# A written engine order replaced as a whole, the first query weights loaded in two pieces, and the last output products split

## The chip, the cores and the metric

The kernel runs on one core of a Trainium2 chip. The core has TensorE (PE, matrix products), VectorE (DVE), ScalarE (ACT), GpSimd (POOL) and SyncE (SP, which here only issues DMAs). The metric is device time in microseconds (us) of one execution, taken as the median of several runs. Alongside, a hardware profiler records one execution: its span runs from the first to the last recorded instruction.

## The reference

Two branches are computed and laid side by side. Branch A is attention with a memory, over 16 heads of width 28 and four segments of 512 rows:

```python
for s in range(N):                       # N = 4 segments, L = 512 rows
    qs, ks, vs = q[:, :, s], k[:, :, s], v[:, :, s]
    logits = jnp.einsum("bhqd,bhkd->bhqk", qs, ks) * scale + mask
    a_dot = jnp.einsum("bhqk,bhkd->bhqd", _softmax(logits), vs)
    pq = phi(qs)                         # phi(t) = t + 1 for t > 0, else exp(t)
    a_mem = einsum(pq, M) / (einsum(pq, z)[..., None] + 1e-6)
    outs.append(g * a_mem + (1.0 - g) * a_dot)      # g = sigmoid(beta)
    pk = phi(ks)
    M = M + jnp.einsum("bhld,bhle->bhde", pk, vs)
    z = z + jnp.einsum("bhld->bhd", pk)
return o @ wo                            # q, k, v = x @ wq, x @ wk, x @ wv
```

Branch B is a state-space convolution of `u` (448 channels, 2048 steps) by FFT, plus `u * D_skip`. All is float32.

## The kernel before, in words

**Units.** Branch A is cut into 16 units: unit t is segment s = t // 4 with a group g = t % 4 of four heads. Every operand of a projection is split into a high and a low part (`wh`/`wl`, `xh`/`xl`), and three products replace one exact one. A projection takes 11 products of 512 columns for the queries and as many for the keys of groups 0 to 2 (`P_proj`, L510), in a part of 6 and a part of 5; a tile of values takes 11 products of 448 columns (`V_tile`, L494).

**A unit's stages.** Score products L584 fill four PSUM banks at a time, in the array's row layout: a fill has blocks of 128 and 256 columns, or 384, or 512. VectorE takes the row maxima from these banks (L592). The maxima are transposed (L599), copied (L600) and written back into the queries. Exponent fills L615, again four banks each, of width 512, 384, and 256 with 128, are read by ScalarE, which makes the exponents P (L619, four instructions per fill); GpSimd sets the part above the diagonal to zero (L622). The products with the values L635 run in the column layout, and ScalarE copies the result (L638). For the memory there are transpositions L551, products L559, the update of M on VectorE (L567, L569) and the product of the mapped queries with M (L537). For the combination, the sums go through DRAM and come back as factors R; multiplications (L713), an addition (L717), a cast to `oh` (L719) and the remainder `ol` (L720) follow, on VectorE for units 13 and 14, on GpSimd for the others. Unit 15 does not go through DRAM: TensorE gathers the sums (L669), VectorE inverts them and applies the gate (L673, L676), TensorE spreads them again (L683, into column layout), and VectorE and ScalarE work in halves (L695 to L702). It does so first for the memory part, then for the dot part.

**Output.** When the four units of a segment are done, each of its four row tiles takes 12 products (`W_tile`, L731): three for each group (`oh` with `wh`, `oh` with `wl`, `ol` with `wh`). ScalarE copies the tile (L737) and SP stores it (L739).

**Branch B.** It runs on the other engines between: 16 tiles, each with a scale on ScalarE (L792), a scan on VectorE (L794), the carried column and the final sum on GpSimd (L796, L799) and a second scale on ScalarE (L797). One buffer, `sc`, serves all the scans. The limits up to which the scan stands for the convolution are worked out on VectorE (L773 to L777), transposed by TensorE (L780) and made a flag; a general convolution behind that flag does not run here.

**What sets the order.** Each operation is recorded with its engine, its buffers and a cost (`Q.op`). The list `ORDER` numbers all of them, and the program is written in exactly that order for every engine and every DMA queue; each engine then takes its own instructions strictly in turn. The recorded costs have no influence on the written order. Buffers are handed out from small pools in the order of the list; the eight PSUM banks (tag `f`) serve everything that TensorE writes, so a fill waits until the engine that reads a bank's earlier contents is through.

**The beginning.** Four products of zeros warm TensorE up (L825). The first input chunks and the first key and query weights are loaded (L449 for weights, L464 for input), cast on ScalarE (L450, L466) and split on VectorE (L453 for weights, L469 and L472 for input). Six small instructions on VectorE (L407 to L412) work out the gates.

## Time and profile before

| | |
|---|---|
| median of 3 runs | 333.07 us (332.98 to 333.58) |
| profiled execution | 333.07 us, span 331.4 us, so 1.67 us lie outside the span |
| TensorE clock granted | 0.998 |
| busy: TensorE, weight loads | 319.6 us (96%), 205.5 us (62%) |
| busy: VectorE, ScalarE, GpSimd | 212.1 us (64%), 217.0 us (65%), 150.1 us (45%) |
| DMA | 36.69 MB, 111 GB/s in the mean |

A matrix product's start is recorded, its end is modelled; since products overlap, the busy time of TensorE is more than the sum of their pitches. In rows of the timeline the first number is the start in us from the span's start, the second the time from the first start to the last end, then engine, line, operation, tiles and count; an idle time before the group and what ended it stand in brackets. In the groups by line the numbers behind the bar are busy time in us, mean ns of one, and idle time before them with its releasers. "PEld" is the load of weights into the array, beside the products.

### The profile page before, as it was taken

The numbers are of one execution on the slowest core, as the hardware profiler recorded it, in microseconds if no ns is written. First come the engines' busy times: TensorE is split into PE (matmuls) and PEld (weight loads), VectorE is DVE, ScalarE is ACT, GpSimd is POOL, SyncE is SP. The second block draws the span as 40 slices with busy tenths as digits, with TensorE's granted clock in tenths as the row PEclk, the third lists the DMA queues.
The fourth block names the chain that finished last, engine by engine and source line by source line (L and its number), as shares of the span: only waits on it lengthen the run. The fifth ranks groups of instructions, "written<-read, shape, count | busy, mean of one in ns | idle before, by whom it ended". The sixth has DMA issues, their size and how long they took to land.

```text
span 331.4 us, 7629 instructions
## 1 busy us (share of the span) xinstructions
PE 319.6 (96%) x2773; PEld 205.5 (62%) x2773; DVE 212.1 (64%) x692; ACT 217.0 (65%) x440; POOL 150.1 (45%) x196
## 2 busy tenths in 40 slices
PE   8999998999899999999999999999999999999992
PEld 3666774756555467657866557566766655557681
DVE  3778778988986887681487567762058368644250
ACT  4555687577788887887747667588533657575531
POOL 4024226446485746745956263534763063270200
PEclk9999999999999999999999999999999999999999
DMA  6665535254452264435542312215350301321203
GB/s 215 238 204 146 168 103 156 81 164 116 131 155 65 85 169 132 143 109 146 152 137 63 94 33 70 88 34 160 89 150 20 108 3 55 106 68 60 93 5 115
DMA packets 25144, 36.69 MB, mean 111 GB/s; under 512 B 7613, under 2 KB 12733, under 8 KB 25101
## 3 DMA queue, kind: packets, MB, share of 16 engines
q1 hardware_dynamic: 24492, 35.48, 36.1%
q10 hardware_dynamic: 608, 0.66, 0.6%
q8 instruction: 24, 0.39, 0.5%
q14 instruction: 20, 0.16, 0.2%
HBM read 21.35 MB, written 14.43 MB: 108 GB/s over the span
## 4 chain that ended last, share of the span: by engine, by line
PE 77%; DMA 5%; issue 4%; ACT 4%; DVE 4%; POOL 4%; ACTq 0%; SPq 0%; POOLq 0%; DVEq 0%
PE f L510 20%; PE f L584 12%; PE f L731 11%; PE f L615 10%; PE f L494 10%; PE f L635 9%; PE f L537 3%; DMA P<-in_wq 2%; POOL P L622 2%; ACT P L619 1%; DMA xin<-in_xT 1%; POOL u L799 1%; PE f L551 1%; DVE sc L794 1%; DVE f L592 1%
## 5 line engine op out<-in xcount | busy, mean ns | idle before, releaser
L592 DVE CUSTOM_DVE_ANT_0 f<-f,mask 128x128 f32<-128x128 f32 (+3 forms) x256 | 119.8, 517 | 57.7 <-PE f L584 56.0
L619 ACT ACTIVATE P<-f 128x384 f32<-128x384 f32 (+1 forms) x192 | 87.0, 534 | 19.3 <-PE f L615 18.3
L622 POOL TENSOR_SCALAR_AFFINE_SELECT P<-P 128x512 f32<-128x512 f32 x64 | 42.1, 671 | 76.6 <-ACT P L619 69.6
L615 PE MATMUL f<-q,k 29*128 29x256 f32 (+3 forms) x512 | 52.1, 460 | 0.6 <-ACT pvn L638 0.4
L584 PE MATMUL f<-k,q 28*128 28x384 f32 (+3 forms) x512 | 49.3, 461 | 0.1
L635 PE MATMUL f<-P,vb 128*32 128x128 f32 (+3 forms) x512 | 37.8, 435 | 1.4 <-POOL xl L469 0.8
L615 PEld LDWEIGHTS f<-q,k 29*128 29x128 f32 x512 | 27.3, 183 | 18.0 <-ACT P L619 6.1
L592 DVE DVE_READ_ACCUMULATOR2_ANT mx<- 128x1 f32 x256 | 36.0, 141 | 0.1
L713 POOL TENSOR_TENSOR pvn<-pvn,R 128x512 f32<-128x512 f32 x22 | 29.7, 1365 | 13.6 <-DMA R<-d 13.6
L635 PEld LDWEIGHTS f<-P,vb 128*32 128x32 f32 x512 | 15.8, 109 | 26.1 <-issue 17.4
L584 PEld LDWEIGHTS f<-k,q 28*128 28x128 f32 x512 | 21.7, 184 | 13.2 <-issue 5.8
L510 PE MATMUL f<-xh,wh_q 128*128 128x512 f32 x64 | 26.9, 420 | 1.1 <-DVE mx L592 0.9
L731 PE MATMUL f<-wh_o,oh 128*128 128x448 f32 x64 | 26.8, 418 | 0.0
L794 DVE TENSOR_TENSOR_SCAN sc<-ones,carry,sc 112x512 f32<-112x512 f32 x16 | 22.8, 1423 | 4.8 <-ACT sc L792 4.6
L494 PE MATMUL f<-wh_v,xh 128*128 128x448 f32 x64 | 25.8, 403 | 0.1
L510 PE MATMUL f<-xh,wl_q 128*128 128x512 f32 x64 | 25.4, 397 | 0.0
L799 POOL TENSOR_TENSOR u<-u,sc 112x512 f32<-112x512 f32 x16 | 20.6, 1285 | 9.5 <-DVE sc L794 4.2
L731 PE MATMUL f<-wh_o,ol 128*128 128x448 f32 x64 | 23.4, 366 | 0.0
L731 PE MATMUL f<-wl_o,oh 128*128 128x448 f32 x64 | 23.4, 366 | 0.0
L494 PE MATMUL f<-wl_v,xh 128*128 128x448 f32 x64 | 23.4, 365 | 0.0
L720 POOL TENSOR_TENSOR ol<-pvn,oh 128x512 fp32r<-128x512 f32 x13 | 16.7, 1281 | 13.7 <-ACT oh L719 13.7
L510 PE MATMUL f<-xh,wh_k 128*128 128x512 f32 x48 | 20.4, 424 | 0.2 <-DVE xh L472 0.2
(134 smaller groups left out, 521.0 us busy)
## 6 DMA issues: line engine op xcount, KB each, us to landing
R<-d SPq DMA_DIRECT2D x44, 128.0 KB
k<-q SPq DMA_DIRECT2D x16, 224.0 KB
u<-in_uT SPq DMA_DIRECT2D x16, 224.0 KB
out_y<-u SPq DMA_DIRECT2D x16, 224.0 KB
out_a<-os SPq DMA_DIRECT2D x16, 224.0 KB
xin<-in_xT SPq DMA_DIRECT2D x12, 256.0 KB
k<-k SPq DMA_DIRECT2D x12, 224.0 KB
P<-in_xT SPq DMA_DIRECT2D x4, 256.0 KB
```

Source lines behind the costliest of these rows:

```text
L494: nc.tensor.matmul(pv.ap, X(s, x, c).ap[:, cs], (wl if w else wh).ap[:, c], start=a, stop=b)
L510: nc.tensor.matmul(pp.ap, (wl if w else wh).ap[:, g, c], X(s, x, c).ap, start=a, stop=b)
L584: nc.tensor.matmul(bank[h].ap[:, c0:c0 + n], q.ap[rows(h), qb * P:(qb + 1) * P], k.ap[rows(h), 0:n], start=True, stop=True)
L592: nc.vector.tensor_tensor_reduce(sc, sc, mask[:, 512 - n:512], 1.0, -3.0e38, ALU.add, ALU.max, mx.ap[:, 4 * h + qb:4 * h + qb + 1])
L615: nc.tensor.matmul(bank[h].ap[:, c0:c0 + w], k.ap[rows(h, 29), kb * P:(kb + 1) * P], q.ap[rows(h, 29), P * kb:512], start=True, stop=True)
L619: Q.op("ACT", act(n), pri + 0.01 * h, lambda h=h: nc.scalar.activation(pb.ap[:, h, 0:n], bank[h].ap[:, 0:n], AF.Exp, scale=SCALE), r=[bank ...
L622: Q.op("POOL", 700, pri + 0.1, lambda c0=c0: nc.gpsimd.affine_select(pb.ap[:, :, c0:c0 + P], pb.ap[:, :, c0:c0 + P], [[0, 4], [1, P]], ALU ...
L635: nc.tensor.matmul(pvp.ap[32 * h:32 * h + 32, kb * P:512], VB(s, kb).ap[:, 4 * g + h, :], pb.ap[:, h, c0:c0 + 512 - P * kb], start=(kb == ...
L713: e.tensor_tensor(pvn.ap[:, i, :], pvn.ap[:, i, :], R.ap[:, 512 * i:512 * i + 512], ALU.mult)
L731: nc.tensor.matmul(po.ap, o.ap[:, cs], w.ap[:, g], start=(g == 0 and i == 0), stop=(g == 3 and i == 2))
L794: Q.op("DVE", 1354, pri, lambda: nc.vector.tensor_tensor_scan(sc.ap, ones.to_broadcast([112, 512]), sc.ap, cj, ALU.mult, ALU.add), r=[sc, ...
L799: Q.op("POOL", 1344, pri, lambda: nc.gpsimd.tensor_tensor(ut.ap, ut.ap, sc.ap, ALU.add), r=[ut, sc], w=[ut])
```

## The change

Three things change in what is recorded. The first query weights come in two loads on ACT's queue, 128 columns and then 384, each with its own cast and subtraction. The two query and key projections of unit 0 are recorded in four parts (3, 3, 3 and 2 products), so that they can alternate. In the last segment's output tiles the three products of unit 15's group become two operations: the two with `oh`, then the one with `ol`. Three recorded costs differ (800 to 700, 870 to 740, 1354 to 1560). The number of recorded operations goes from 1493 to 1504; TensorE's products are the same in number and shape. And the list `ORDER` is replaced from the first number to the last.

```diff
 ORDER = """
-73 0 11 1 2 8 23 5 14 20 21 54 17 22 27 42 12 24 74 13 30 3 45 4 48 9 10 6 102 7 55 56 15 98 16 18 19 28 103 29 99
+26 57 0 14 2 73 5 1 11 72 75 8 17 23 74 20 24 30 25 27 58 59 15 45 16 3 48 6 4 51 12 7 107 13 9 54 101 10 55 108 18
...
-        def load_w(nm, i, pri, eng="DVE", at=None, by="SP"):
+        def load_w(nm, i, pri, eng="DVE", at=None, by="SP", cs=range(4)):
             hi, lo = W[nm]
-            n = 512 if nm in "qk" else D
+            c0, n = P * cs[0], P * len(cs) if nm in "qk" else D
...
+            part = lambda z: flat(z.ap[:, i])[:, c0:c0 + n]
+            b, key = t if isinstance(t, tuple) else (t, 0)
+            t = (b, (key, c0)) if len(cs) < 4 else t
+            raw = lambda: b.ap[:, 512 * key + c0:512 * key + c0 + n]
+            at = [(i, c) for c in cs] if nm in "qk" else [i]
+            Q.op(by, 430, pri, lambda: (nc.sync if by == "SP" else nc.scalar).dma_start(raw(), src()[:, c0:c0 + n]), w=[t], land=-4 * P * n)
+            Q.op("ACT", act(n), pri, lambda: nc.scalar.copy(part(hi), raw()), r=[t], w=[(hi, a) for a in at])
...
-        def product(s, cost, pri, one, reads, out, hold):
-            for ii in (PASSES[0:6], PASSES[6:11]):
+        def product(s, cost, pri, one, reads, out, hold, cuts=(0, 6, 11)):
+            for ii in (PASSES[x:y] for x, y in zip(cuts, cuts[1:])):
...
-            product(s, r32(512), pri, one, [(wh, g), (wl, g)], pp, [d])
+            product(s, r32(512), pri, one, lambda cs: [(w, (g, c)) for w in (wh, wl) for c in cs], pp, [d],
+                    (0, 3, 6, 9, 11) if t == 0 else (0, 6, 11))
...
             for g in range(NG):
                 r = [] if s == 3 else [*st[4 * s + 3]["o"]]
-                r += [(o, lt // 2) for o in st[4 * s + g]["o"]]
-                Q.op("PE", 3 * r32(448), pri, lambda g=g: part(g), r=[(wh, g), (wl, g), *r], w=[po],
-                     hold=[os], mode="full")
+                oh, ol = ((o, lt // 2) for o in st[4 * s + g]["o"])
+                for ii, o in (((0, 1), [oh]), ((2,), [ol])) if 4 * s + g == 15 else (((0, 1, 2), [oh, ol]),):
+                    Q.op("PE", len(ii) * r32(448), pri, lambda g=g, ii=ii: part(g, ii), r=[(wh, g), (wl, g), *r, *o], w=[po],
+                         hold=[os], mode="full")
...
-            Q.op("DVE", 1354, pri, lambda: nc.vector.tensor_tensor_scan(
+            Q.op("DVE", 1560, pri, lambda: nc.vector.tensor_tensor_scan(
...
-        load_w("q", 0, -8.95, at=(z1, 0), by="ACT")
+        load_w("q", 0, -8.97, at=(z1, 0), by="ACT", cs=range(1))
+        load_w("q", 0, -8.95, at=(z1, 0), by="ACT", cs=range(1, 4))
```

Below, the places of the new list that matter here. A row gives its number on the engine, the line (those of the changed kernel lie 3 to 8 further on), the operation, what is written and what is read, with buffer numbers, and the size of what is written; `f_67` to `f_74` are the eight banks.

**The beginning, on VectorE.** `xh`/`xl` 78 to 81 and 86 to 88 are the four input chunks, `gt`, `ga`, `omg` and `mix` the gates. Before:

```order
3 L453 TENSOR_TENSOR wl_k<-P_102,wh_k 128x512
4 L375 TENSOR_REDUCE sel_155<-sel 128x1
5 L469 TENSOR_TENSOR xl_86<-P_101,xh_78 128x512
6 L469 TENSOR_TENSOR xl_87<-P_101,xh_79 128x512
7 L453 TENSOR_TENSOR wl_q<-P_102,wh_q 128x512
8 L407 TENSOR_SCALAR gt<-gt 128x20
9 L408 RECIPROCAL gt<-gt 128x20
10 L409 TENSOR_SCALAR ga<-gt 128x20
11 L410 COPY omg<-ga 128x4
13 L412 SCALAR_TENSOR_TENSOR mix<-mix,sel_155,omg 128x4
14 L469 TENSOR_TENSOR xl_88<-P_101,xh_80 128x512
15 L472 TENSOR_TENSOR xh_81<-P_101,xh_81 64x512
```

Now:

```order
3 L407 TENSOR_SCALAR gt<-gt 128x20
5 L408 RECIPROCAL gt<-gt 128x20
8 L411 TENSOR_TENSOR mix<-gt,omg 128x4
9 L412 SCALAR_TENSOR_TENSOR mix<-mix,sel_155,omg 128x4
10 L456 TENSOR_TENSOR wl_k<-P_102,wh_k 128x512
11 L472 TENSOR_TENSOR xl_86<-P_101,xh_78 128x512
12 L456 TENSOR_TENSOR wl_q<-P_102,wh_q 128x128
13 L472 TENSOR_TENSOR xl_87<-P_101,xh_79 128x512
14 L456 TENSOR_TENSOR wl_q<-P_102,wh_q 128x384
15 L472 TENSOR_TENSOR xl_88<-P_101,xh_80 128x512
16 L475 TENSOR_TENSOR xh_81<-P_101,xh_81 64x512
```

The gate instructions moved ahead of all splits, and the split of the first query weights is in two. On SP's queue, the gates' input moved to the head from behind the first three input chunks, the two loads of `ld` and `ds` that stood at the head moved behind the weights, and the four input chunks follow one another. TensorE takes key and query products of the same chunk alternately.

**Exponent fills, on TensorE.** L615 (now L620) are exponent fills, L584 (L589) score fills, L731 (L737) output products, L559 (L564) memory products. Unit 13 before:

```order
1162 L615 MATMUL f_67<-q_91,k_95 128x128
1163 L615 MATMUL f_71<-q_91,k_95 128x128
1164 L615 MATMUL f_74<-q_91,k_95 128x128
1165 L615 MATMUL f_70<-q_91,k_95 128x128
1166 L615 MATMUL f_68<-q_91,k_95 128x384
1167 L615 MATMUL f_72<-q_91,k_95 128x384
1168 L615 MATMUL f_71<-q_91,k_95 128x384
1169 L615 MATMUL f_74<-q_91,k_95 128x384
1170 L584 MATMUL f_69<-k_96,q_92 128x512
1171 L584 MATMUL f_70<-k_96,q_92 128x512
1172 L584 MATMUL f_73<-k_96,q_92 128x512
1173 L584 MATMUL f_67<-k_96,q_92 128x512
```

Unit 13 now, from behind the memory products that follow its 128 and 256 wide fill:

```order
1170 L737 MATMUL f_68<-wh_o,oh_111 128x448
1171 L737 MATMUL f_68<-wl_o,oh_111 128x448
1172 L737 MATMUL f_68<-wh_o,ol_116 128x448
1173 L620 MATMUL f_74<-q_91,k_95 128x512
1174 L620 MATMUL f_73<-q_91,k_95 128x512
1175 L620 MATMUL f_72<-q_91,k_95 128x512
1176 L620 MATMUL f_70<-q_91,k_95 128x512
1177 L737 MATMUL f_68<-wh_o,oh_112 128x448
1178 L737 MATMUL f_68<-wl_o,oh_112 128x448
1179 L737 MATMUL f_68<-wh_o,ol_117 128x448
1180 L589 MATMUL f_71<-k_96,q_92 128x384
1181 L589 MATMUL f_67<-k_96,q_92 128x384
```

Between the fills now stand output products, and the 384 wide one has moved behind the score fill. Unit 5 now, from the middle of its 128 and 256 wide fill on:

```order
491 L620 MATMUL f_68<-q_91,k_95 128x128
492 L620 MATMUL f_70<-q_91,k_95 128x128
493 L620 MATMUL f_72<-q_91,k_95 128x384
494 L620 MATMUL f_69<-q_91,k_95 128x384
495 L620 MATMUL f_73<-q_91,k_95 128x384
496 L620 MATMUL f_67<-q_91,k_95 128x384
497 L589 MATMUL f_70<-k_96,q_92 128x512
498 L589 MATMUL f_68<-k_96,q_92 128x512
499 L589 MATMUL f_71<-k_96,q_92 128x512
500 L589 MATMUL f_67<-k_96,q_92 128x512
501 L556 MATMUL f_72<-ident,phk_99 128x128 x4
502 L620 MATMUL f_69<-q_91,k_95 128x512
```

Here two exponent fills, a score fill and a transposition stand together; before, unit 5 had a 384 and a 512 wide exponent fill and a 128 and 256 wide score fill in a row.

**The end, on TensorE.** `oh`/`ol` 108 and 113 belong to unit 15; L669 (L674) gathers, L683 (L688) spreads. Before, for the dot part:

```order
1306 L731 MATMUL f_71<-wh_o,oh_111 128x448
1307 L731 MATMUL f_71<-wl_o,oh_111 128x448
1308 L731 MATMUL f_71<-wh_o,ol_116 128x448
1309 L669 MATMUL f_72<-pick,pvn_105 128x4 x4
1310 L731 MATMUL f_67<-wh_o,oh_111 128x448
1311 L731 MATMUL f_67<-wl_o,oh_111 128x448
1312 L731 MATMUL f_67<-wh_o,ol_116 128x448
1313 L683 MATMUL f_69<-ident,rr_133 32x128 x16
1314 L731 MATMUL f_68<-wh_o,oh_111 128x448
```

Now:

```order
1318 L737 MATMUL f_68<-wh_o,oh_111 128x448
1319 L737 MATMUL f_68<-wl_o,oh_111 128x448
1320 L737 MATMUL f_68<-wh_o,ol_116 128x448
1321 L674 MATMUL f_69<-pick,pvn_105 128x4 x4
1322 L688 MATMUL f_67<-ident,rr_133 32x128 x16
1323 L737 MATMUL f_74<-wh_o,oh_112 128x448
1324 L737 MATMUL f_74<-wl_o,oh_112 128x448
```

The three output products between gather and spread are gone from there. Behind the spread stand 24 output products instead of 33; twelve of the last 15 belong to unit 15, each two with `oh_108` followed by the one with `ol_113`.

**The limits, on VectorE.** The five instructions L773 to L777 (L780 to L784) stood between the maxima of unit 4's 384 wide and 512 wide score fills; now they stand among the four maxima of unit 5's 512 wide score fill. On TensorE the transposition of their result (L780, now L787) follows the second exponent fill of unit 3 behind that.

20 lines of the change are left out of this document (9 added, 11 removed), and 110 rows, old and new, of the table ORDER.

## The prediction

> **What bounds the kernel now.** I read the page first (busy shares, clock, chain), then TensorE's waits, then its timeline beside that of the engine it waits for.
>
> ```profile
> PE 319.6 (96%) x2773; PEld 205.5 (62%) x2773; DVE 212.1 (64%) x692; ACT 217.0 (65%) x440; POOL 150.1 (45%) x196
> ...
> PEclk9999999999999999999999999999999999999999
> ...
> PE 77%; DMA 5%; issue 4%; ACT 4%; DVE 4%; POOL 4%; ACTq 0%; SPq 0%; POOLq 0%; DVEq 0%
> ```
>
> TensorE is busy 96% at full clock and carries the chain; the others reach 65%. So the time is TensorE's own stream plus the holes in it. The 319.6 us overstate the stream: a product's modelled end lies after the start of the next, so part of a hole counts as busy. I therefore measure starts, not ends. The timeline of TensorE at one such hole (start, duration, engine, line, operation, tiles, count):
>
> ```profile
> 83.61 0.40 PE L510 MATMUL f<-xh,wl_k 128*128 128x512 f32 x1
> 83.94 1.14 PE L584 MATMUL f<-k,q 28*128 28x512 f32 x8
> 84.90 1.40 PE L615 MATMUL f<-q,k 29*128 29x512 f32 x8
> 87.20 0.50 PE L510 MATMUL f<-xh,wh_q 128*128 128x512 f32 x1 [0.90 <-DVE mx L592]
> 87.54 0.40 PE L510 MATMUL f<-xh,wl_q 128*128 128x512 f32 x1
> 87.77 0.40 PE L510 MATMUL f<-xl,wh_q 128*128 128x512 f32 x1
> ```
>
> and of VectorE there:
>
> ```profile
> 84.20 1.11 DVE L773 TENSOR_TENSOR mxa<-mxa,mxb 112x4 f32<-112x4 f32 x1
> ...
> 86.40 0.69 DVE L592 CUSTOM_DVE_ANT_0 f<-f,mask 128x512 f32<-128x512 f32 x1
> ```
>
> Eight score products of 512 columns fill four banks in 0.96 (83.94 to 84.90). The next eight, alike, are followed only after 2.30 (84.90 to 87.20), so 1.34 is lost, though only 0.90 is shown as idle. VectorE had 2.20 of scan-limit arithmetic (84.20 to 86.40) in front of a row maximum that empties a bank. The rows also price a change of array layout: within projections the pitch is 0.23 (87.54 to 87.77), but 0.33 into a score fill (83.61 to 83.94) and 0.34 after the return (87.20 to 87.54): 0.10 + 0.11 = 0.21 for each.
>
> Such holes, read the same way, are what an order can win: I find about 13.9 us, of which the parts below name the larger. The stream without them, which the change does not shorten except by layout changes, stays.
>
> **The start.** TensorE's first products and, below them, VectorE in the same stretch:
>
> ```profile
> 7.01 0.60 PE L510 MATMUL f<-xh,wh_k 128*128 128x512 f32 x1
> ...
> 11.59 0.50 PE L510 MATMUL f<-xh,wh_k 128*128 128x512 f32 x1 [0.22 <-DVE xh L472]
> ...
> 13.33 0.40 PE L510 MATMUL f<-xh,wh_k 128*128 128x512 f32 x1
> ```
>
> ```profile
> 8.86 0.17 DVE L407 TENSOR_SCALAR gt<-gt 128x20 f32<-128x20 f32 x1
> ...
> 10.13 0.68 DVE L469 TENSOR_TENSOR xl<-P,xh 128x512 fp32r<-128x512 f32 x1
> 10.84 0.69 DVE L472 TENSOR_TENSOR xh<-P,xh 64x512 fp32r<-64x512 f32 x1
> ```
>
> The first 22 products take 6.32 (7.01 to 13.33); at 0.233 each they need 5.13. The 1.19 lost lie just before the row at 11.59, where VectorE is still at the splits of the third and fourth input chunk because six gate instructions ran from 8.86 to 10.13 ahead of them. These six now come first, before any data has landed; their input, formerly fifth on SP's queue, heads it, and the two tiny scan loads no longer stand before the input chunks. The 128-column load costs one more DMA issue on ACT's queue, one short cast and one short subtraction, a few tenths in time those engines have spare; its earlier landing buys nothing by itself, since the warm-up products hold TensorE to about 7. I take the full -1.2; bounds 0 (a chunk lands late) and -1.5.
>
> By the page "TensorE: Matmul & The Clock Gate", section Back-to-back issue gap, 512 columns need about 216 ns in isolation. With it the 22 products would take 4.75 and this term would be -1.57. The row says 233 ns, and the row decides.
>
> **Layout changes.** Counted in both orders, 155 become 153: -0.4 at 0.21 each; bounds -0.6 and 0. The page "TensorEngine Tiling (Array Packing)", section Key Properties, says that changing tiling mode drains TensorE, and "TensorE: Matmul & The Clock Gate", Single matmul latency, gives a constant of about 0.17 us; two would then be worth 0.34. The trace agrees that a change costs something.
>
> **The limits.** They move off the place above, which frees 1.34. But now they stand between the first two and the last two maxima of a later 512-wide fill, and the short transposition of their result follows on TensorE, ahead of projections for the values. From that fill's start VectorE needs two maxima (0.69 at most), 2.20 of limits and another maximum, some 4.6 with the start-up; TensorE has 4.64 of work until there (0.96 fill, two-part projection 2.78, 0.03, 0.87 score fill), but the scan before the fill starts VectorE late by nearly a microsecond. New hole 0.9 (bounds 0, 1.8): net -0.45.
>
> **Fills drawn apart.** Three stretches of before (197 to 203, 275 to 278, 288 to 291) have two or three exponent fills with little between. The last of them on TensorE, and ScalarE in the middle one:
>
> ```profile
> 288.31 2.46 PE L615 MATMUL f<-q,k 29*128 29x384 f32 x22
> 290.93 0.47 PE L731 MATMUL f<-wh_o,oh 128*128 128x448 f32 x1
> ```
>
> ```profile
> 276.09 3.17 ACT L619 ACTIVATE P<-f 128x384 f32<-128x384 f32 x8 [0.92 <-PE f L615]
> ```
>
> ScalarE needs 0.38 for each 384-wide exponent (seven steps of 0.38 and a last 0.50 make the 3.17), TensorE about 0.7 for a fill that feeds four of them. Two fills in a row put 3 us on ScalarE behind 1.4 us of TensorE; the next fill finds its banks full. At 288.31 two fills worth 1.40 take 2.62: 1.22 lost. Summed the same way, the other two lose 1.4 and 1.5. In the new order, output products of 0.6 to 0.8 stand between these fills (the order's excerpt on unit 13); the same count leaves 0.5, 0.35 and 0.1. Gain 4.1 - 0.95, taken as -3.2; bounds -4.1 and -1.5.
>
> **Unit 5.** Here the new order does what it avoids elsewhere: 128/256 and 384 exponent fills, then a 512 score fill.
>
> ```profile
> 120.55 2.26 PE L615 MATMUL f<-q,k 29*128 29x384 f32 x15
> ...
> 124.12 0.47 PE L731 MATMUL f<-wh_o,oh 128*128 128x448 f32 x1
> ```
>
> From the groups by line and shape (count, busy total, mean ns, idle before and its releasers):
>
> ```profile
> L713 POOL TENSOR_TENSOR pvn<-pvn,R 128x512 f32<-128x512 f32 x22 | 29.7, 1365 | 13.6 <-DMA R<-d 13.6
> ...
> L792 ACT ACTIVATE sc<-u,c0t 112x512 f32<-112x512 f32 x16 | 11.6, 728 | 4.2 <-POOL carry L796 2.4 <-POOL u L799 1.1 <-DMA u<-in_uT 0.6
> ...
> L638 ACT COPY pvn<-f 128x512 f32<-128x512 f32 x16 | 9.3, 584 | 13.5 <-PE f L635 13.1 <-issue 0.5
> ```
>
> Before: 3.57 (120.55 to 124.12) for fills worth 2.36, so 1.2 lost. After: from the end of the value products ScalarE has a copy (0.58), a scale (0.73) and a relu, priced like the copy (0.3 less for all three, since one starts before the other's modelled end), then five exponents of 0.38 before the score fill has its first bank: 3.5, with start-ups 3.85. TensorE brings three fills of about 0.7. Lost 1.8, and 0.3 in the output products behind: +0.9; bounds 0 and +2.
>
> **Small rest.** The same count finds two shortfalls, 0.34 and 0.2, where before has none: +0.5; bounds 0 and +1.5. Gaps of before that no single queue explains are not credited.
>
> **The tail.**
>
> ```profile
> 315.55 1.05 PE L669 MATMUL f<-pick,pvn 128*128 128x4 f32 x8
> 316.46 0.45 PE L731 MATMUL f<-wh_o,oh 128*128 128x448 f32 x1
> ...
> 317.25 1.08 PE L683 MATMUL f<-ident,rr 128*32 128x128 f32 x32
> ...
> 324.77 0.37 PE L731 MATMUL f<-wh_o,ol 128*128 128x448 f32 x1
> ```
>
> Gather to spread takes 1.70 (315.55 to 317.25): gather products, reciprocal and gate factor on VectorE, then the spread. In it stands one output tile's 0.79 (316.46 to 317.25). The new order has the spread directly after the gather, so about 0.8 becomes a hole; the tile is done elsewhere. What follows shrinks from 33 output products to 24, and the chain from the spread to the last unit's first half must still fit: spread 1.08 and nine products of 0.2 cover 2.9; two multiplications and a sum of half width on VectorE and a cast on ScalarE need about as much. The split lets the first two products of a tile go before the low part is there; price without that cover 0.4. +0.8; bounds +0.3 and +1.3. Last copy and store stay as they are.
>
> **Sum.** -1.2 - 0.4 - 0.45 - 3.2 + 0.9 + 0.5 + 0.8 = -3.05. The profiled execution is 333.07, the median of the runs 333.07 as well: 330.0, span 328.3.
>
> **Rivals.** (1) *Given back* (0.15): the holes move rather than close. For it: before, 3.1 of 13.9 us of holes were of a kind that no single queue explains; against it, the start's 1.2 is plain. With the limits at 1.8, half the fill gain and unit 5 at +2: -1.2 - 0.4 + 0.45 - 1.6 + 2 + 0.5 + 0.8 = +0.55; taken 333.1 to 333.6, no change. (2) *Slower* (0.14): the scale instruction L792 waits for the one scan buffer, which GpSimd frees after a sum of its own, itself queued behind 1.37 products (L713, 22 of them); ScalarE then stands with exponents behind it and TensorE without banks. Before, its six such waits (2.4 + 1.1) hit little. In unit 5 it stands directly before eight exponents with about 0.5 to spare. One delay of a GpSimd product costs 1.37; from three of the 16 tiles on (4.1) it decides: 334.1. (3) *Order better than I count* (0.15): unit 5 and the tail take no more than before and the limits hide: -1.2 - 0.4 - 1.34 - 3.2 = -6.1, with the small rest 327.5. (4) *The split does nothing*: true already in my sum for the load; if input chunks land late too, the start gives 0 and the time is 331.2, inside the forecast's range.
>
> **Numbers.** Forecast 0.56 (own range 328.3 to 331.9). Likeliest 330.0; 8 in 10 from 327.4 to 333.8. 0.2%, or 0.67 us, is about what a measurement here tells from no change: faster 0.73 (forecast, better, and the edge of given back), same 0.12, slower 0.15.
>
> **What will show it.** Start: the 23rd product at 12.1 rather than 13.33. Limits: no hole near 85, one of about 0.9 at the flag's transposition. Units 9, 13, 14: exponents in fours of 1.64 with output products between. Unit 5: a hole of 1.8. Tail: spread 1.7 after gather with nothing between, last product 6.0 after that spread. Wrong if holes in the middle sum to more than 9 us, above all behind L792.

## The result

Over 20 runs each on one chip the kernel before takes 333.4 us (median) and the changed kernel 331.48 (330.58 to 334.74); the ratio is 0.9949, with a 95% interval of 0.9926 to 0.9971. So it is faster by about 1.7 us, with 1.0 to 2.5 as the interval (the medians lie 1.9 apart). On another chip, beside the last experiments, the unaltered changed kernel gave 331.97 and 0.9938 [0.9917, 0.9959]. Three of the 20 runs had a granted clock of 0.984 or 0.985 where the others had 0.994 to 0.998, and took 334.2 to 334.7.

The profiled execution took 331.92, span 330.2. Its page answers to the one of before as follows (busy time by engine, TensorE's granted clock over 40 slices, shares of the chain that ended last):

```profile
PE 316.8 (96%) x2773; PEld 205.4 (62%) x2773; DVE 216.6 (66%) x693; ACT 216.5 (66%) x441; POOL 151.8 (46%) x196
...
PE 82%; DVE 7%; ACT 4%; DMA 3%; issue 1%; POOL 0%; ACTq 0%; SPq 0%; POOLq 0%
```

TensorE carries more of the chain (82% for 77%), VectorE is busy 4.5 us longer although it got one small instruction more. The places where TensorE waits, from the view of waits of the changed kernel (engine, line, awaited engine, tile and line: total, times, longest):

```profile
PE f L514 <- POOL xh L475: 1.7, 1, 1.7
...
PE f L787 <- DVE mx L597: 1.3, 1, 1.3
PE f L620 <- DVE mx L597: 0.6, 1, 0.6
PE f L688 <- DVE rr L681: 0.6, 1, 0.6
```

These show the projections waiting for an input chunk, the flag's transposition, unit 5's exponent fills and the last spread. (Line numbers are now 3 to 7 higher: the maxima L592 are L597, the exponents L619 are L624, the products L713 and L720 are L718 and L725, the scale L792 is L799, the scan L794 is L801, the tiles' sum L799 is L806, the limits L773 to L777 are L780 to L784.)

Holes measured as in the prediction, start to start less the stream's own pitch, give this balance of the two profiled executions, one of each kernel:

| place | forecast | holes before | holes after | measured |
|---|---|---|---|---|
| start | -1.2 | 1.2 | 0.4, and the first product 0.2 later | -0.6 |
| layout changes (content of the stream) | -0.4 | | | -0.5 |
| limits | -0.45 | 1.34 | 1.35 | 0.0 |
| fills of units 9, 13, 14 | -3.2 | 4.1 | 0.9 | -3.2 |
| unit 5 | +0.9 | 1.2 | 2.6 | +1.4 |
| tail | +0.8 | 0.35 | 0.85 | +0.5, and 0.1 less behind the last product |
| all the rest | +0.5 | | | +1.3 |
| span | -3.05 | 331.4 | 330.2 | -1.2 |

The rest holds two numbers of opposite sign: 1.9 us at a place that has no hole before (the input chunk), and 0.6 us by which the other gaps shrank on balance. So the fills gain 3.2 and everything else together gives 2.0 of it back. That the two fewer layout changes are worth 0.5 is counted from the pitches; no run tries it by itself.

The largest forecast term came as worked out. Unit 14's last fills, TensorE and below it ScalarE:

```profile
287.07 0.82 PE L620 MATMUL f<-q,k 29*128 29x384 f32 x8
288.17 0.47 PE L737 MATMUL f<-wh_o,oh 128*128 128x448 f32 x1 [0.27 <-DVE mx L597]
```

```profile
287.96 1.64 ACT L624 ACTIVATE P<-f 128x384 f32<-128x384 f32 x4 [1.07 <-PE f L620]
```

A fill of eight stands alone now, exponents come in fours of 1.64, output products follow, and 0.35 is left of a hole of 1.22. No run moves these fills alone, but the reading repeats: the three stretches last 6.02, 3.60 and 2.61 us in both traces of the old order there (the kernel before and its variant with a new start, below), and where they stand in the new order, with the products between, 5.24, 4.36 and 4.33, the same to 0.02 us in all twelve traces of it.

### The profile page after: what moved, and what is told of

Same layout as the page of the kernel before. It is cut to its first block, busy times and chain, and to the rows that moved or that the text cites. A ratio compares the mean times of both kernels' runs of the same rounds, so it can differ in the third digit from the quotient of the medians.

```text
span 330.2 us, 7639 instructions
## 1 busy us (share of the span) xinstructions
PE 316.8 (96%) x2773; PEld 205.4 (62%) x2773; DVE 216.6 (66%) x693; ACT 216.5 (66%) x441; POOL 151.8 (46%) x196
## 4 chain that ended last, share of the span: by engine, by line
PE 82%; DVE 7%; ACT 4%; DMA 3%; issue 1%; POOL 0%; ACTq 0%; SPq 0%; POOLq 0%
PE f L514 20%; PE f L737 13%; PE f L589 11%; PE f L498 11%; PE f L620 10%; PE f L640 9%; DMA xin<-in_xT 3%; PE f L542 3%; DVE f L597 3%; ACT P L624 2%; PE f L832 2%; DVE sc L801 2%; PE f L556 2%; PE f L564 1%; PE f L688 1%
## 5 line engine op out<-in xcount | busy, mean ns | idle before, releaser
L597 DVE CUSTOM_DVE_ANT_0 f<-f,mask 128x256 f32<-128x256 f32 (+3 forms) x256 | 120.2, 514 | 58.4 <-PE f L589 56.6
L624 ACT ACTIVATE P<-f 128x384 f32<-128x384 f32 (+1 forms) x192 | 87.0, 532 | 18.3 <-PE f L620 16.9
L627 POOL TENSOR_SCALAR_AFFINE_SELECT P<-P 128x512 f32<-128x512 f32 x64 | 43.9, 699 | 85.4 <-ACT P L624 85.0
L620 PE MATMUL f<-q,k 29*128 29x256 f32 (+3 forms) x512 | 49.6, 459 | 0.6 <-DVE mx L597 0.6
L589 PE MATMUL f<-k,q 28*128 28x512 f32 (+3 forms) x512 | 48.7, 458 | 0.0
L620 PEld LDWEIGHTS f<-q,k 29*128 29x128 f32 x512 | 26.2, 183 | 16.5 <-issue 8.0
L597 DVE DVE_READ_ACCUMULATOR2_ANT mx<- 128x1 f32 x256 | 35.7, 140 | 0.1
L801 DVE TENSOR_TENSOR_SCAN sc<-ones,carry,sc 112x512 f32<-112x512 f32 x16 | 24.7, 1546 | 9.8 <-ACT sc L799 9.5
L718 POOL TENSOR_TENSOR pvn<-pvn,R 128x512 f32<-128x512 f32 x22 | 28.9, 1330 | 4.3 <-DMA R<-d 4.3
L589 PEld LDWEIGHTS f<-k,q 28*128 28x128 f32 x512 | 21.9, 184 | 13.0 <-issue 7.1
L806 POOL TENSOR_TENSOR u<-u,sc 112x512 f32<-112x512 f32 x16 | 21.0, 1310 | 14.5 <-DVE sc L801 7.3
L737 PE MATMUL f<-wh_o,oh 128*128 128x448 f32 x64 | 26.8, 419 | 0.3 <-DVE mx L597 0.3
L725 POOL TENSOR_TENSOR ol<-pvn,oh 128x512 fp32r<-128x512 f32 x13 | 16.7, 1287 | 14.9 <-ACT oh L724 13.2
L737 PE MATMUL f<-wh_o,ol 128*128 128x448 f32 x64 | 23.4, 366 | 0.0
L737 PE MATMUL f<-wl_o,oh 128*128 128x448 f32 x64 | 23.3, 365 | 0.0
```

Source lines behind the costliest of these rows:

```text
L589: nc.tensor.matmul(bank[h].ap[:, c0:c0 + n], q.ap[rows(h), qb * P:(qb + 1) * P], k.ap[rows(h), 0:n], start=True, stop=True)
L597: nc.vector.tensor_tensor_reduce(sc, sc, mask[:, 512 - n:512], 1.0, -3.0e38, ALU.add, ALU.max, mx.ap[:, 4 * h + qb:4 * h + qb + 1])
L620: nc.tensor.matmul(bank[h].ap[:, c0:c0 + w], k.ap[rows(h, 29), kb * P:(kb + 1) * P], q.ap[rows(h, 29), P * kb:512], start=True, stop=True)
L624: Q.op("ACT", act(n), pri + 0.01 * h, lambda h=h: nc.scalar.activation(pb.ap[:, h, 0:n], bank[h].ap[:, 0:n], AF.Exp, scale=SCALE), r=[bank ...
L627: Q.op("POOL", 700, pri + 0.1, lambda c0=c0: nc.gpsimd.affine_select(pb.ap[:, :, c0:c0 + P], pb.ap[:, :, c0:c0 + P], [[0, 4], [1, P]], ALU ...
L718: e.tensor_tensor(pvn.ap[:, i, :], pvn.ap[:, i, :], R.ap[:, 512 * i:512 * i + 512], ALU.mult)
```

## What held VectorE: the limits once more

In the changed kernel the limits stand at 95.77, and the flag's transposition waits for the maxima behind them. VectorE and GpSimd there:

```profile
95.77 1.60 DVE L780 TENSOR_TENSOR mxa<-mxa,mxb 112x4 f32<-112x4 f32 x1
97.29 0.15 DVE L781 TENSOR_TENSOR sai<-sai,sar 112x4 f32<-112x4 f32 x1
97.48 0.48 DVE L782 SCALAR_TENSOR_TENSOR lim<-mxa,sai 112x4 f32<-112x4 f32 x1
```

```profile
96.05 1.30 POOL L725 TENSOR_TENSOR ol<-pvn,oh 128x512 fp32r<-128x512 f32 x1
97.29 0.66 POOL L627 TENSOR_SCALAR_AFFINE_SELECT P<-P 128x512 f32<-128x512 f32 x1
```

An addition over 112 x 4 numbers takes 1.60, the next one of the same size 0.15. The long one ends at 97.37 where GpSimd's L725 ends (97.35), the third ends at 97.96 with GpSimd's L627 (97.95). In the kernel before it was the same, which the prediction did not look at. VectorE's second row there, and GpSimd:

```profile
85.24 0.66 DVE L774 TENSOR_TENSOR sai<-sai,sar 112x4 f32<-112x4 f32 x1
```

```profile
84.03 1.27 POOL L799 TENSOR_TENSOR u<-u,sc 112x512 f32<-112x512 f32 x1
85.25 0.63 POOL L622 TENSOR_SCALAR_AFFINE_SELECT P<-P 128x512 f32<-128x512 f32 x1
```

L773 (84.20 + 1.11) ends with L799 (84.03 + 1.27), L774 with L622. So the 2.20 of the prediction's "scan-limit arithmetic" was mostly waiting. The longest case in the changed kernel is a scan that takes 1.28 elsewhere:

```profile
109.50 3.54 DVE L801 TENSOR_TENSOR_SCAN sc<-ones,carry,sc 112x512 f32<-112x512 f32 x1
```

```profile
108.23 1.30 POOL L718 TENSOR_TENSOR pvn<-pvn,R 128x512 f32<-128x512 f32 x1
109.47 1.22 POOL L627 TENSOR_SCALAR_AFFINE_SELECT P<-P 128x512 f32<-128x512 f32 x2
110.66 1.29 POOL L725 TENSOR_TENSOR ol<-pvn,oh 128x512 fp32r<-128x512 f32 x1
```

GpSimd works without a gap until 111.95; the scan ends 1.09 later, about its own length. It began beside one GpSimd instruction, and three more were served before it. The instructions concerned (scans, limits, the factors rc, the mapped queries and keys) read two operands from SBUF; the maxima L597, which read a PSUM bank and a mask, are not lengthened beside GpSimd (the 64 of 128x512 take 0.67 to 0.73). Summed over all VectorE instructions that are more than 0.2 us above the usual length of their line and shape, the loss is 10.3 us before (17 instructions) and 14.2 after (20); the difference is most of VectorE's extra 4.5. In all 37 cases a GpSimd instruction was running when the long one began.

The Trainium skill, page "SBUF — State Buffer", section Who interferes with whom, says that a VectorE instruction with two SBUF inputs contends with a GpSimd instruction that reads SBUF, that contention for the shared ports is an exclusive lock, and (of VectorE's two-port modes) that whoever issues first has the ports for its whole instruction while the other is blocked fully. The trace agrees on the lock, with 1.60 for 0.15 and 3.54 for 1.28. It goes beyond the page in that one instruction lost to four in a row.

## Experiments

All are measured against the kernel before on the same chip. The edits of the order are shown as the numbers of the list, with the operation in brackets. In the altered versions of the changed kernel the line numbers are lower by one.

**The limits elsewhere.** The three operations (98 the limits, 99 the transposition, 100 the flag) move to a stretch in which VectorE is nearly idle.

```diff
-460 954 98 305 875 ... 463 555 99 472 ... 474 100 471
+1174 1119 98 1181 1184 ... 1187 1139 99 1051 ... 1059 1054 100 1026
```

> The changed kernel with the five limit instructions moved to a stretch near 225 us in which VectorE is nearly idle, and the transposition and the flag behind them. Traces so far: the five took 2.49 us in the changed kernel (L780 1.60, L782 0.48, each ending together with a GpSimd instruction) and 2.20 before; TensorE then waited 1.3 us at the transposition. Theory 'port' (a VectorE instruction with two inputs in SBUF stands until the GpSimd instruction beside it ends): the hole of 1.3 near 97 us closes, and the five take under 1.0 us where GpSimd is idle, more only where one of its instructions overlaps. Theory 'work' (their time is their own arithmetic and start-up): they take 2.2 to 2.5 us there too; the hole closes as well. Both: span about 1.0 us shorter than the changed kernel's 330.2, unless the maxima behind them were waiting for something else.

VectorE with the limits at their new place:

```profile
232.20 0.16 DVE L779 TENSOR_TENSOR mxa<-mxa,mxb 112x4 f32<-112x4 f32 x1
```

The five instructions take 0.15 to 0.16 each and 0.81 from the first start to the last end, instead of 2.58. The lock explains them; arithmetic does not. The hole at the transposition is gone. The time is 330.93, ratio 0.989 [0.9844, 0.9935] from five runs. In the profiled one the clock fell after unit 5, so its span of 331.7 says nothing on the gain.

**GpSimd's product behind the scan.** GpSimd's L725 (407) goes behind the carried column (1033), so that it no longer passes the scan at 109.5.

```diff
-407 [POOL ol] ... 562 1033 [POOL carry] 480
+... 562 1033 [POOL carry] 407 [POOL ol] 480
```

> The changed kernel with one GpSimd instruction moved: the low part of unit 2 (L725, which ran 110.66 to 111.95 us) stands behind the carried column of the scan that began at 109.50 and took 3.54 us, so it cannot run beside this scan. Nothing is changed on VectorE. Theory 'port': the scan now ends when the two selections end (110.69) plus its own 1.28, so it takes 2.4 instead of 3.54, the row maxima of unit 6 come 1.1 us earlier, and of the 2.6 us of holes around the exponent fills of unit 5 about 1.0 goes. Rival 'ScalarE' (as the prediction had it: unit 5's holes come from the copy, scale, relu and exponents on ScalarE): the scan's length does not matter, the holes stay within 0.3 of 2.6.

VectorE there, and one line of the waits:

```profile
109.06 2.27 DVE L800 TENSOR_TENSOR_SCAN sc<-ones,carry,sc 112x512 f32<-112x512 f32 x1
...
111.51 1.33 DVE L655 TENSOR_SCALAR rc<-rc,omg 128x16 f32<-128x16 f32 x1
...
115.58 1.54 DVE L530 SCALAR_TENSOR_TENSOR phq<-phq,relu 128x512 f32<-128x512 f32 x1
```

```profile
PE f L619 <- DMA q<-mr: 1.2, 1, 1.2
```

The scan falls from 3.54 to 2.27, by the 1.27 of one GpSimd product. But the product now holds L655 (1.33 where 0.24 is usual), and the tiles' sum holds L530 (1.54 where 0.69 is). The lock went to the next instruction, and TensorE then waited for the DMA that carries the row of maxima. Unit 5's holes grew to 3.4, which neither theory expected; the time is 333.25, ratio 1.0002 [0.9965, 1.0039].

**The fourth chunk first.** In the changed kernel the keys' projection stops for the fourth input chunk of segment 2. SP's queue, ScalarE's cast and the stopped product:

```profile
148.43 0.37 SPq L746 DMA_DIRECT2D out_a<-os  x1
149.25 0.59 SPq L651 DMA_DIRECT2D rc<-pvn  x1
149.96 0.40 SPq L467 DMA_DIRECT2D xin<-in_xT  x1
```

```profile
155.53 0.62 ACT L469 CAST xh<-xin 128x512 fp32r<-128x512 f32 x1 [2.48 <-DMA xin<-in_xT]
```

```profile
157.60 0.50 PE L514 MATMUL f<-xh,wh_k 128*128 128x512 f32 x1 [1.67 <-POOL xh L475]
```

The chunk's fetch (682) stood on SP behind an output store and behind a fetch that waits for ScalarE's copy. It is issued no later than in the kernel before, whose fetch and cast of the same chunk are these:

```profile
150.11 0.33 SPq L464 DMA_DIRECT2D xin<-in_xT  x1
```

```profile
154.04 0.64 ACT L466 CAST xh<-xin 128x512 fp32r<-128x512 f32 x1
```

But TensorE now needs the chunk at 155.77 instead of 157.86, and its cast starts 1.5 us later. How long the stop is differs: from the product before it is 2.06 here, and 1.06 to 1.55 in the seven other traces that leave this place as it is. The edit:

```diff
-679 [SP xin] ... 509 [SP out_a] 820 761 [SP rc] 828 682 [SP xin]
+679 [SP xin] ... 682 [SP xin] 509 [SP out_a] 820 761 [SP rc] 828
```

> The changed kernel with one DMA moved on SP's queue: the load of the third segment's fourth input chunk, issued at 149.96 us behind a store and the fetch of unit 6's sums (which waits for ScalarE's copy), stands ahead of both. Theory 'queue': it is issued as soon as its buffer is free, about 148.9, lands before the spread of the factors shares the DMA engines, and the hole of 1.9 us at 155.8 (TensorE waiting for GpSimd's L475 on this chunk) falls under 0.8. Rival 'GpSimd' (the split waits for its turn on GpSimd): issue earlier, hole unchanged. Rival 'buffer': the load waits for a free input buffer and is issued as late as before; the hole stays and the store and fetch come later.

SP's queue and, below it, TensorE at the same products:

```profile
147.53 1.18 SPq L466 DMA_DIRECT2D xin<-in_xT  x2
```

```profile
155.09 0.40 PE L513 MATMUL f<-xl,wh_k 128*128 128x512 f32 x1
155.32 0.40 PE L513 MATMUL f<-xh,wh_k 128*128 128x512 f32 x1
```

The stop is gone: the product that stood 2.06 behind its forerunner now follows after 0.23. The span is 328.4, 1.8 less: 0.36 of it lies ahead of the 23rd product, and 0.5 of what the stop cost is lost again at 232, where keys wait for exponents. The time is 330.42, ratio 0.9899 [0.9857, 0.9941] from four runs. So one moved fetch gives nearly as much again as the whole change, though the interval still touches that of the changed kernel.

**A tile in the last gather.** One output tile (1477) goes between gather (1458) and spread (1460), as in the kernel before.

```diff
-1484 1419 1435 1477 [PE output] 1434 ... 1458 [PE gather] 1422 1459 1423 1460 [PE spread]
+1484 1419 1435 1434 ... 1458 [PE gather] 1477 [PE output] 1422 1459 1423 1460 [PE spread]
```

> The changed kernel with one group of three output products moved from ahead of the last memory product to between the last gather and the last spread. Theory of the prediction (1.7 us from gather to spread, of which only 0.9 is work): the hole of 0.70 before the spread falls to about 0.1, and the span shortens by 0.5 to 0.7, since the covers the products leave have slack. Rival: the products were covering something where they stood, and a hole of the same size opens at the first spread or at the value products of unit 15; no change.

The changed kernel, then this one, at the last spread:

```profile
316.25 1.06 PE L674 MATMUL f<-pick,pvn 128*128 128x4 f32 x8
317.86 1.08 PE L688 MATMUL f<-ident,rr 128*32 128x128 f32 x32 [0.56 <-DVE rr L681]
```

```profile
317.39 1.08 PE L687 MATMUL f<-ident,rr 128*32 128x128 f32 x32
```

From gather to spread it is 1.61 with nothing between, and the wait is gone with a tile there: the span falls by 0.6. The time, 332.19 and 0.996 [0.9933, 0.9987], cannot be told from the changed kernel's.

**The start, from three sides.** The first loads the first query weights in one piece, the second leaves out one of the four warm-up products, the third is the kernel *before* with only the new start of the order (gate load first, gates early, scan loads later).

```diff
-        load_w("q", 0, -8.97, at=(z1, 0), by="ACT", cs=range(1))
-        load_w("q", 0, -8.95, at=(z1, 0), by="ACT", cs=range(1, 4))
+        load_w("q", 0, -8.95, at=(z1, 0), by="ACT")
```

> The changed kernel with the first query weights in one load, cast and subtraction again; all else in its order. Theory of the prediction (the split load buys nothing, the gate instructions and the order of the input loads do): the 23rd product starts within 0.15 of 5.53 us after the first (7.20 to 12.73 in the changed kernel), no stop of TensorE in between beyond the 0.39 behind the first product. Rival (the split is what feeds TensorE): the fifth product, which needs the low part of the first query weights, stops for 0.4 us or more, and the distance grows to 5.9 or more.

```diff
-WARM = 4
+WARM = 3
```

> The changed kernel with three warm-up products instead of four. In the runs so far the first product started at 6.90 to 7.20 us whenever its input was cast (the cast ended at 6.5 to 7.0), and it always took 0.60 instead of 0.23 to the next. Theory 'warm-up holds': the first product starts at the end of the first cast, about 6.6, the third waits for the low part of the first chunk (7.3), and the 23rd starts at 12.0 to 12.4 instead of 12.73. Rival 'clock': with less work ahead, TensorE is not yet at full clock when the products begin; several run at half pace (0.43 from one to the next) and the 23rd comes at 12.7 or later. The span moves by as much in either case.

```diff
-73 [SP scan] 0 11 1 2 8 23 5 14 20 21 54 [SP gates] 17 ... 42 12 24 74 13 ... 7 55 56 [DVE gates] 15
+54 [SP gates] 0 11 1 2 8 23 5 14 20 21 17 ... 42 55 12 24 56 [DVE gates] 13 ... 48 73 [SP scan] 9 ... 43 74
```

> The kernel before with only the beginning changed: gates' input at the head of SP's queue, the two tiny loads of the scan behind the weights, the gate instructions ahead of the splits on VectorE and their exponent first on ScalarE. No split load, TensorE's order as before. Theory: this is all that the start of the change is worth: the two stops of 0.73 in all at the third and fourth input chunk go, the 0.37 behind the first product stays, so the 23rd product starts 5.5 us after the first (6.32 before), and the time falls by 0.5 to 0.8. The prediction's number would be 5.13 after the first. Rival: the stops come from the order of TensorE's own products (keys of two chunks, then queries) and stay.

From the first to the 23rd product it is 6.32 in the kernel before, 5.53 in the changed one, 5.52 with one load, 5.49 with three warm-up products and 5.61 in the kernel before with the new start. So by this distance the early gates are worth 0.7 to 0.8 and the split load nothing (331.86, one run). The distance also depends on when the input lands: with the limits late and with the three repairs below, which leave the start alone, the second chunk's cast ends about a microsecond later (8.83 and 8.63 for 7.59), and it is 5.95 and 5.97. The 23rd product starts at 12.1 to 13.1 in the thirteen traces with the new start, and at 13.33 in the one of the kernel before. What is left is seen in the changed kernel's first two products, 0.63 apart where 0.23 is the pitch; no run shows why:

```profile
7.20 0.79 PE L514 MATMUL f<-xh,wh_k 128*128 128x512 f32 x1
7.83 0.39 PE L514 MATMUL f<-xh,wl_k 128*128 128x512 f32 x1
```

The first chunk's cast there ends at 6.57, and the first product follows only at 7.20, without a gap behind the warm-up:

```profile
5.95 0.62 ACT L469 CAST xh<-P 128x512 fp32r<-128x512 f32 x1 [1.52 <-DMA P<-in_xT]
```

With three warm-up products the first product comes no earlier, but the input landed later in that run, the cast ended at 7.16, and the product waits for it:

```profile
7.21 0.50 PE L513 MATMUL f<-xh,wh_k 128*128 128x512 f32 x1 [0.39 <-ACT xh L468]
```

So this run cannot tell what the fourth warm-up product costs: in the changed kernel's trace the warm-up held TensorE, here the data did. Its time is 331.78, ratio 0.9939 [0.9915, 0.9963], the changed kernel's own. The kernel before with the new start gave 334.29, 0.9993 [0.9965, 1.002]: gained at the start, the time was lost again in the middle, where two holes of 0.54 and 0.40 had opened (at 129 and 136).

**Unit 5's fills in turn.** The second exponent fill (642) goes ahead of the first score fill (614), so that exponent and score fills alternate.

```diff
-357 614 [PE scores] 580 426 1128 ... 642 [PE exponents] ... 646 ... 643 ... 644 ... 645
+357 642 [PE exponents] 580 646 643 644 645 614 [PE scores] 426 1128 ...
```

> The changed kernel with the 384-wide exponent fill of unit 5 moved ahead of the 128/256-wide score fill of unit 6, and its four exponents directly behind the copy of unit 4's values, so that score and exponent fills alternate there. Theory 'ScalarE' (the prediction's: two exponent fills in a row put eight exponents on ScalarE while TensorE has nothing else): the holes around unit 5, 2.6 us in the changed kernel, fall to about 1.0. Rival 'VectorE' (the row maxima are late there because VectorE is held up by GpSimd: 3.54 us for a scan of 1.28): the holes stay at 2 or more, only at other fills, since VectorE is 95% busy from 105 to 120 us.

One row of TensorE, then the busy times by stretches of 5 us (PE, PEld, DVE, ACT, POOL, granted clock, DMA share, GB/s):

```profile
117.35 0.93 PE L619 MATMUL f<-q,k 29*128 29x384 f32 x8 [1.14 <-DMA q<-mr]
```

```profile
115.00:120.00 5.00, 3.86 (x53) 2.48 (x46) 3.38 (x15) 3.33 (x8) 1.27 (x1) 0.95 0.61 167
120.00:125.00 5.00, 5.00 (x25) 2.97 (x23) 4.25 (x18) 2.79 (x7) 1.89 (x3) 0.50 0.28 85
125.00:130.00 5.00, 5.00 (x46) 2.08 (x45) 1.89 (x7) 3.31 (x7) 2.43 (x3) 0.52 0.39 101
```

The fill brought forward now waits for the DMA of its row of maxima, whose way the score fill had covered: 1.3 lost where the changed kernel loses nothing. Behind it TensorE's granted clock falls to half for about ten us, and the holes there (1.7 and 2.0) hold the slower clock as well. The time is 335.48, ratio 1.005 [1.0016, 1.0084]: slower than before. How much ScalarE's queue costs here it does not tell; that what is relieved there is lost at the DMA it does.

**Three repairs together**: the limits late, the fourth chunk first and the tile in the gather, edited as above.

> The changed kernel with three repairs at once: the limits' five small instructions at the stretch in which VectorE is idle (after 230), the fourth chunk's fetch ahead of the store and the rc fetch on SP's queue, the last tile's copies in the gather. If each place is its own stop, the savings add up: 1.35 at the limits, 1.93 at the projection's chunk and .70 at the last spread, 3.5 to 4 off the span of 330.2, so 326.5 and a time near 328. If what is saved at one place is spent again at the next crowded one (unit 5, where VectorE is nearly always busy), the time is that of the fetch put first alone, 330 to 330.5.

All that is left of TensorE's waits of 0.3 us and more:

```profile
PE f L831 <- DVE pvn L393: 1.5, 1, 1.5
PE f L563 <- DVE mx L596: 0.3, 1, 0.3
```

The first is the wait of the warm-up for its zeros; two more rows are like the second. (The view shows idle time alone: by starts, unit 5 still holds its 2.6.) The span is 326.9, 3.3 less than the changed kernel's on that chip. The first product comes 0.7 earlier (6.80 instead of 7.49), which no repair explains, but by the 23rd only 0.24 of that is left (12.78 instead of 13.02). So 3.1 remain of the 3.5 that the three stops cost there (1.35, 1.41 and 0.70). The time is **329.12** (328.59 to 332.12), ratio **0.9874 [0.9837, 0.9912]**, against 0.9938 for the changed kernel beside it. About nine tenths of the savings add up in the profiled execution; in the medians the gain on the changed kernel is 2.9. This is the fastest order of the case.

**The scan tiles elsewhere.** Tiles 9 to 15 of branch B move, so that no scan stands ahead of unit 5 any more (tile 9 from 109.5 to 126); once alone, once with the three repairs.

```diff
-tiles 9 to 15, scans at 109.5 125.9 130.1 145.1 160.3 166.8 177.8
+tiles 9 to 15, scans at 126.3 131.0 137.0 146.7 152.1 163.0 167.0
```

> The changed kernel with its B-tiles 9 to 15 moved: tile 9 with its scan from 109.5 to 126, 10 to 130, 11 to 137, 13 from 160 to 150, 14 to 156 and 15 to 161, nothing else. If unit 5's holes of 2.63 come from VectorE being held beside GpSimd (a scan of 3.54 there, and of 1.28 where GpSimd doesn't run), the stretch from 106 to 121 loses the scan and most of its holes: 1.0 or less is left, and the time is 330.0 or below. If the holes come from the order of the dealing itself, or if the lock finds the next two-input instruction of VectorE as it did when only the product was moved, the holes stay above 2 and the time stays at 331.5.

> The three repairs and the moved tiles together. If they are separate stops: the span falls by 5 to 5.5 from 330.2 and the time is 326.5 to 327.5, with no hole over .6 between 60 and 300. If savings are spent again behind each place: 330 or above.

> The changed kernel itself, unaltered, on the chip on which the three others run, as their common yardstick: 331.5 and a ratio of 0.995 if the first measurement holds; every theory expects the same of it.

Alone it takes 339.68, ratio 1.0167 [1.0135, 1.0199]; with the repairs 333.21, 0.9994 [0.9967, 1.002]. Both are about 4 to 8 us worse than without the move. VectorE and TensorE at unit 5, with the tiles moved alone:

```profile
109.76 2.22 DVE L655 TENSOR_SCALAR rc<-rc,omg 128x16 f32<-128x16 f32 x1
```

```profile
117.93 1.53 PE L619 MATMUL f<-q,k 29*128 29x256 f32 x18 [0.86 <-DMA q<-mr]
```

Without the scan, L655 takes its place in front of the same GpSimd instructions (2.22 where 0.24 is usual). VectorE still comes free more than a microsecond earlier and then idles, and TensorE waits for the DMA of the maxima instead. Unit 5's holes are 3.1 with the tiles moved alone, and with the repairs, where that DMA is in time, 2.3 (0.52, 0.57 and 1.19). In the changed kernel they are 2.66 on that chip, the last two again 0.57 and 1.19. So the lock is worth 0.4 at most there. The last two belong to the order of the fills. Of these, the changed kernel's trace names the emptying engines, VectorE's maxima for the second fill and ScalarE's exponents for the third (weight loads and products):

```profile
118.53 1.37 PE L620 MATMUL f<-q,k 29*128 29x384 f32 x6 [0.58 <-DVE mx L597]
...
120.83 0.29 PEld L589 LDWEIGHTS f<-k,q 28*128 28x128 f32 x2 [0.47 <-ACT P L624]
```

Where the moved tiles went, they cost more than the stop they left. TensorE's longest wait, GpSimd's splits of two earlier chunks, the fetches of the third and fourth chunk on SP and the cast of the fourth, with the tiles moved alone:

```profile
PE f L513 <- POOL xh L474: 4.5, 1, 4.5
```

```profile
150.88 2.51 POOL L471 TENSOR_TENSOR xl<-xin,xh 128x512 fp32r<-128x512 f32 x2
```

```profile
152.17 0.33 SPq L466 DMA_DIRECT2D xin<-in_xT  x1
...
155.04 0.36 SPq L466 DMA_DIRECT2D xin<-in_xT  x1
```

```profile
161.36 0.62 ACT L468 CAST xh<-xin 128x512 fp32r<-128x512 f32 x1 [4.28 <-DMA xin<-in_xT]
```

The fourth chunk's fetch went from 149.96 to 155.04. Most of that lies ahead of the third chunk's fetch (152.17 instead of 147.97): SP stands there from 149.0 on, until the first of GpSimd's two splits, which now follow a moved tile's sum, frees an input buffer. The tile's own store and load on SP add 0.9 between the two fetches. With the fetch first (the repairs) that stop is 0.6, but TensorE still waits 1.4 for a select on GpSimd, as it does with the tiles moved alone:

```profile
146.90 1.50 POOL L626 TENSOR_SCALAR_AFFINE_SELECT P<-P 128x512 f32<-128x512 f32 x1 [3.42 <-ACT P L623]
```

Here GpSimd is the one that stands: 1.50 instead of 0.64, beside the moved scan of 146.70 to 147.98 (and 1.50 again with the repairs). The lock works both ways. It accounts for 0.9; the select also started 2.2 later than in the changed kernel (144.66), since its exponents came later.

## Why the prediction was right, and where it was not

The time (331.48) lies in the forecast's own range and the direction was right; of a gain of 3.05 some 1.7 came. It lies near the edge of the range (331.9), where the profiled execution (331.92) and the median on the other chip (331.97) fall just outside.

**Fills drawn apart: right**, in mechanism and size (-3.2 of -3.2). It carries the whole result. The other terms nearly cancel in the forecast (+0.15), but measured they give back 2.0, above all at the input chunk, which the forecast did not have, and at unit 5. That the time still fell inside the range is owed to its width.

**Layout changes: as counted** (-0.5 for -0.4), with no run that isolates them.

**The start: right mechanism, term mis-sized.** The early gates end the stop at the third and fourth chunk, as said, but the step that called all of the 1.19 "just before the row at 11.59" lumped in 0.4 directly behind the first product, which stays. It is -0.8 from first to 23rd product, and -0.6 in absolute time (12.73 instead of 13.33; forecast 12.1), since the first product came 0.2 later, a difference that arises without a change there (6.4 to 7.5 over the kernels here). That the split load buys nothing was right. That "the warm-up products hold TensorE" was right of the changed kernel's trace (0.63 behind the cast's end); in eight of the fourteen traces the first product starts 0.05 or 0.06 behind the cast instead.

**The limits: the step failed that took 2.20 for arithmetic.** The instructions need 0.8 in all; the rest was GpSimd's lock, and it was there to be read in the rows of before beside GpSimd's. With the cause unseen, the new hole came out at 0.9 and measured 1.35, so the term is 0 for -0.45. The bounds (0 to 1.8) held it. Read rightly, the row would have said: the cost depends on what GpSimd does beside it.

**Unit 5: mechanism partly right, term mis-sized.** Three fills in a row outrun the engines that empty their banks; the holes sum to 2.6 instead of 2.1, +1.4 for +0.9. The forecast's single cause, ScalarE's queue, stands behind the third hole only; the second waits for VectorE's maxima. The experiment that put the fills in turn made it worse, since the DMA of the maxima ends next. Three chains end here close together: VectorE's maxima, that DMA (2.6 to 4.0 us from its issue to the fill behind it) and ScalarE's exponents.

**The tail: right mechanism, slightly too dear** (hole of 0.70 at the spread, forecast 0.8; +0.5 for +0.8).

**The small rest: the step failed that let "gaps of before that no single queue explains" stand and saw only 0.54 of new ones.** Several of those gaps closed or shrank. In their place came 1.9 at the fourth chunk of segment 2, which the prediction missed because it followed TensorE and the engines but not SP's queue: the fetch stands there behind a store and another fetch, is issued no later than in the kernel before, but TensorE needs it 2.1 us sooner. One moved fetch shows it.

**The rivals.** *Given back* came in part: +1.4 at unit 5, 0 at the limits, 1.9 at the chunk; not enough to decide. *Slower* did not come: ScalarE's scale has less idle time before it than in the kernel before (4.2 there), and in unit 5, at 117.05, none at all.

```profile
L799 ACT ACTIVATE sc<-u,c0t 112x512 f32<-112x512 f32 x16 | 11.7, 729 | 3.1 <-POOL u L806 0.9 <-POOL carry L803 0.7 <-POOL ol L725 0.7
```

It looked for GpSimd's cost in a buffer that comes free late. GpSimd's cost was in VectorE's instructions. *Better than counted* was the size of what an order can still win: with three places mended, the measured gain is 4.5 us in the medians (333.65 to 329.12), where the forecast had 3.05 and that rival 5.6.

**The sign of being wrong** named for the middle, holes of more than 9 us in all, was set too low to decide anything. By the prediction's own 13.9, less 1.2 at the start and 0.35 at the tail, the middle held 12.3 before, and its forecast would have left 10.1; by the balance above some 12 are left, and no wait of TensorE's products names the scale (now L799).

What stays open: why the fill behind the DMA of the row of maxima starts 2.6 to 3.0 us after its issue in the orders in which it does not wait for it, and 3.05 to 3.97 in the four in which it does. It was not tried by itself. Open is also why the chunk's stop differs between traces of the same order (2.06 and 1.53).

## What to carry to other kernels

When an instruction takes several times its usual length in one place, put the other engines' rows beside it before calling it work: a small VectorE instruction that takes long and ends within a few hundredths of a microsecond of a GpSimd instruction has been waiting for it, and belongs where GpSimd is idle. Judge a new order queue by queue, the DMA queues too; the costliest new stop was one input fetch that stood behind a store and another fetch while TensorE came to need it sooner. Mend the separate stops first, since those add up; to empty the busiest stretch by moving work elsewhere cost more than it gave, because other chains ended there at nearly the same time.

## What the runs showed of the hardware

- VectorE's instructions on two SBUF operands and GpSimd's lock each other out for whole instructions, several in a row: a 112 x 512 scan took 3.54 instead of 1.28, an addition over 112 x 4 numbers 1.60 instead of 0.15, and a GpSimd select 1.50 instead of 0.64.
- TensorE's granted clock was seen to halve behind holes that follow each other closely, though none is long; that the holes cause it is not shown. With the fills in turn, TensorE was busy for 3.86 of the 5 us from 115 to 120, and the granted clock was 0.50 in the next five and 0.52 in the five behind. With the limits late it was busy for 4.57 of the same 5 us, and the clock was 0.54 from 120 to 125. But it stayed at 1.00 behind 4.42 in the changed kernel's profiled run, and behind 4.14 with the tiles moved. So the busy share alone does not decide. The Trainium skill, page "TensorE: Matmul & The Clock Gate", section What's actually happening, has the clock fall after an idle window of about 3.4 us that runs free of the kernel; the holes ahead of these falls are not that long (1.3 at most). With the tiles moved TensorE stood for 4.47 us at the fourth chunk, and there the trace agrees: the clock was 0.50 from 164 to 167. Its section A second HAM failure mode: psum-queue depth-cycling says that frequent short idle times between groups of products are enough to make the clock swing, and the falls behind unit 5's short holes fit that one. The free-running window would fit a fall in some runs only (3 of the 20 of the changed kernel); no run here shows it.
